# Top-32 attention with a channel mix: the mix cut into eighteen chunks of 256 rows instead of nineteen of four sizes, and the last batch walked in two passes over its heads instead of three

## The chip, the cores and the metric

The kernel runs on one core of a Trainium2 chip. The metric is device time in microseconds (us). The time before is the median of three runs; beside it stands one execution that was recorded by the hardware profiler. A core has TensorE (PE, matmuls; PEld is its weight load, which overlaps), VectorE (DVE), ScalarE (ACT), GpSimd (POOL) and SyncE (SP, which here only issues transfers).

## The reference, cut to what matters

```python
# B, H, S, D = 8, 8, 576, 64; d_model 512, d_ff 1024; all float32
scores = (q @ k.T) / 8                      # per batch and head, 576 x 576
kth    = 32nd largest of each row
attn   = softmax(where(scores >= kth, scores, -1e9))
x      = concat over heads of attn @ v      # B x 576 x 512
x_prev = x shifted down by one row, zero first
xk, xr = mu_k*x + (1-mu_k)*x_prev, mu_r*x + (1-mu_r)*x_prev
k      = relu(xk @ w_k)                     # 512 -> 1024
out    = sigmoid(xr @ w_r) * ((k*k) @ w_v)  # 1024 -> 512
```

`w_k`, `w_v`, `w_r`, `mu_k`, `mu_r` are shared by all batches; some of them arrive in 64 bits.

## The kernel before, in words

**Attention.** Heads go in four pairs `hp` of a batch. A pair's queries are cut into tiles numbered 0 to 8: tiles 0 to 7 come two by two (128 query rows for two heads), tile 8 holds the last 64 rows of both heads. That makes 288 tiles for 8 batches. For each tile PE computes scores (`score`, `sliver`, or `score8`, lines 957 to 974), ACT copies them out (`keep`), DVE finds the 32nd largest value with short maxima (`cand`, `best`, `drop`, `eighth`, `nine`) with the help of one ACT pass (`count`) and one POOL pass (`below`), ACT takes the exponential, DVE masks (`mask`), PE transposes (`turn`, `turnl`), ACT copies out, PE multiplies with v (`weigh`, L1048 and L1049), and DVE writes the normalised result into `xT[b]` (`place`, L1079 for two units of 128 rows at once, L1081 for one unit or for tile 8).

**Visits.** `visits()` lists (batch, pair, tiles). Normally a batch is walked in two passes, `HALVES = range(4), range(4, 9)`: tiles 0 to 3 of all four pairs, then tiles 4 to 8 of all four. `EDGE` gives the last batch three passes: tiles 0 to 3, 4 to 7, and 8 alone. Each visit loads and transposes the left-over rows (`load_t`, L898; `turn_t`, L930; `cr`, L932) and loads v (L903, L906). K itself is kept from one pass to the next (`HOLD`).

**Mix.** The 4608 rows (8 x 576, batches one after another) are cut into chunks by `SIZES`; a chunk may reach over a batch's end. For a chunk of n rows, POOL and ACT build the mixed inputs (`change` L1151, `share` L1156, `add` L1161, `xh` L1163, `xl` L1165), once for k and once for r, in two halves of two head pairs each. Every product runs as three matmuls, high by high, high by low, low by high (`three`, L688 to L690). `hidden` (L1172) puts weights in the array and moves n columns: 8 blocks x 4 x 3 = 96 matmuls per chunk, whatever n is. `relu`, `sq` (ACT), `r2`, `hl` (POOL) follow each pair of blocks. `gate` and `value` move 512 columns with up to 128 rows of the chunk as weights: 12 and 24 matmuls for each piece of up to 128 rows, so a chunk of 192 rows pays for two pieces. After the gates come `gexp` (ACT), `ga` (POOL L1199), `ln`, `inv1` (ACT), `newton` (POOL L1202), and after the values `scaled` and `gated` (DVE) and the store. In the last chunk `scaled` doesn't need the values (L1213).

**Which rows a chunk waits for.** `need` (L1133) lists the units of `xT` a chunk reads. Unit u is rows 128u to 128u+127 of a batch.

**Weights.** The 20 blocks of 128 x 512 are converted from 64 bits into a high and a low part (`weight`, L1236): one ACT, four DVE, two more ACT and one POOL step, and then for the first 12 blocks three-term sums on PE (`wsub`, with `ident` and a constant tile `minus`, the negative identity) and a copy on ACT (`wlo`), for the last 8 (the `v` blocks) two steps on POOL (L1270, L1271).

**Order.** Nothing is issued in program order. `Plan.op` registers each step with an engine, a cost and a key (a tile number plus `OFF[name]`, plus `HEAD[name]` for keys under `EARLY` = 48 and `TAIL[name]` for keys over `LATE` = 252); `Plan.run` plays the engines forward with these costs and picks on each engine the smallest key among the steps that can start soon. The result is a fixed order for every engine. A chunk's keys start at the later of 15.812 tiles per 256 rows after the chunk before and 10.811 tiles after the tile that completes its rows (lines 1128 to 1132). `piece` (L1120) chains all mix matmuls in order of chunks, and holds each until enough tiles have been scored.

```python
SIZES = [256] * 15 + [192, 256, 192, 128]
HALVES = range(4), range(4, 9)
EDGE = {B - 1: (range(4), range(4, 8), range(8, 9))}
```

Of the kernel before, what the change touches and what calls it, by code (L numbers as in the profile page):

```python
# [37 lines left out]
OFF = dict(kt=-21.783, kq=-11.008, rest=-13.373, v=-2.634, v8=10.138, tk=-6.089, ck=8.262, tq=-5.225, cq=-6.43, tr=-1.237, cr=-7.526, zero=22.403,  # L38
           score=-0.141, score8=-15.038, keep=-1.452, cand=4.806, best=-7.531, drop=-27.471, under=-2.738, nb=0.767, count=2.416, below=0.769,
           eighth=5.912, nine=7.69, exps=3.127, mask=1.266, turn=3.431, et=4.216, turnl=3.572, el=4.446, weigh=1.287, inv=2.357, inv2=-3.109,  # L40
           turni=-0.324, ri=1.01, place=-2.072, lowest=19.594, ranks=8.879, mu=-9.778, nmu=10.655, changek=8.233, sharek=-1.743, addk=-14.153,
           xhk=-0.414, xlk=-27.681, changer=-6.404, sharer=6.926, addr=3.569, xhr=6.702, xlr=-7.161, hidden=2.099, relu=-12.166, sq=4.501, r2=5.634,
           hl=-5.112, gate=1.899, gexp=6.101, ga=13.942, ln=-1.538, inv1=3.806, newton=-6.724, value=-0.034, scaled=-16.811, gated=-14.314,
           store=4.14, w=20.061, wabs=-2.342, wclamp=0.949, wshift=-6.042, wsign=-2.057, wexp=-2.168, wfine=1.502, whi=3.775, wmul=5.552,
           wsub=-10.606, wlo=3.473, spread=1.98, sliver=-2.472, low=4.289, lowt=-10.047, lowr=-8.942, lowc=-1.374)
# [21 lines left out]
SIZES = [256] * 15 + [192, 256, 192, 128]  # L67
# [4 lines left out]
BONUS = {("S", "W"): -0.314, ("T", "W"): 3.274, ("R", "W"): 3.937, ("T", "S"): -0.018, ("R", "S"): -0.24, ("W", "S"): -1.276, ("S", "R"): 1.995, ("T", "R"): -0.982, ("W", "R"): 4.176, ("R", "R"): -0.147}  # L72
# [331 lines left out]
def topk_attention_channel_mix(ctx: ExitStack, tc: tile.TileContext, q, k, v, mu_k, mu_r, w_k, w_v, w_r, out):  # L404
# [8 lines left out]
    minus = consts.tile([128, 128], F32R, name="minus")  # L413
    nc.vector.tensor_scalar(minus, ident, -1.0, None, op0=OP.mult)
# [7 lines left out]
    nmu = consts.tile([128, 2, HP], F32, name="nmu")  # L422
# [433 lines left out]
    def attend(plan, visits, X, pair_sums):  # L856
# [8 lines left out]
        for p, (b, hp, part) in enumerate(visits):  # L865
# [11 lines left out]
            P.q = {i: (buf("qn"), buf("qs")) for i in part if i % 4 == 0 and i < 8}  # L877
# [47 lines left out]
            for i, (qn, qs) in P.q.items():  # L925
                turned(qn, 2, lambda c, qn=qn: flat(qn.t[:, c]), "q", lambda qs=qs: qs.t, qs, at0 + i - P.first, fast=soon and i == 0)
# [14 lines left out]
            for i in part:  # L941
# [80 lines left out]
                if i % 2 or i == 8:  # L1022
# [28 lines left out]
                    plan.op(PE_, "weigh", n, cost, cost + 197, weigh, reads=[t.et for t in es] + [el] + [P.v, P.vr if i < 8 else P.vr8], writes=[U.pa[u]], mode="W")  # L1051
# [184 lines left out]
    def weight(plan, X, name, which, block, hi, lo, n):  # L1236
# [25 lines left out]
        if n < WPE:  # L1262
            pl = buf("rot")

            def rest():
                return [nc.tensor.matmul(pl.t, lhsT=minus if i == 1 else ident, rhs=x, start=i == 0, stop=i == 2) for i, x in enumerate((val.t, hi, fine.t))]
            plan.op(PE_, "wsub", key, 2050, 2250, rest, reads=[val, fine, (W, ('h', which))], writes=[pl], mode="T")
            done.append(plan.op(ACT, "wlo", key, 520, 630, lambda: nc.scalar.activation(lo, pl.t, AF.Copy), reads=[pl], writes=[(W, which)]))
        else:
# [147 lines left out]
```

## Time and profile before

| what | value |
|---|---|
| time, median of three runs | 1258.56 us (1258.01 to 1259.78) |
| the profiled execution's own time | 1260.28 us |
| its span | 1258.4 us |
| PE busy | 1204.9 us (96%) |
| DVE busy | 1136.3 us (90%) |
| ACT busy | 1114.2 us (89%) |
| POOL busy | 986.4 us (78%) |
| mean granted TensorE clock | 0.977 |

The span runs from the first to the last instruction on record; the time of the same execution is 1.88 us longer. Busy shares are means over a start in which weights are converted, a long stretch in which attention and mix run together, and an end in which only the mix is left, so they are to be read by stage. A matmul's recorded duration includes its way through the array; where matmuls follow one another, the distance between their starts is what each costs.

### The profile page before, as it was taken

To read this page: it belongs to the slowest core of one execution; us is meant where nothing else is said; L and a number is where in the kernel's file an instruction comes from. 1 tells how busy PE (TensorE), PEld (TensorE's weight loads), DVE (VectorE), ACT (ScalarE), POOL (GpSimd) and SP (SyncE) were. 2 spreads that over 40 slices of the span, in tenths; PEclk is the share of its full clock that TensorE was granted. 3 is DMA by queue.
4 is the path that set the end of the run, shared out by engine and by line. 5 is a ranking of instruction groups with operands and counts; after the bars stand their busy time and mean duration, and the time that the engine had idled before them with its cause. 6 is when DMAs were issued, how large, how long until landed. Compare 5 with 4: busy or idle time off the path is not lost.

```text
span 1258.4 us, 29994 instructions
## 1 busy us (share of the span) xinstructions
PE 1204.9 (96%) x9205; PEld 926.6 (74%) x9205; DVE 1136.3 (90%) x6219; ACT 1114.2 (89%) x2455; POOL 986.4 (78%) x885
## 2 busy tenths in 40 slices
PE   5786999999999999999999999999999999999998
PEld 3344777877777777777787877787878787778786
DVE  5999999999999999999999999999999999999101
ACT  5798899999999999999999999999999899999442
POOL 2558995987788887887888797978788879788783
PEclk8897799999999999999999999999999999999999
DMA  6233112111221112011211121112210211110100
GB/s 185 83 101 95 37 35 64 40 37 39 58 55 35 38 38 74 24 50 44 70 36 38 36 58 49 40 29 61 54 39 28 59 49 44 31 40 26 42 18 24
DMA packets 127257, 62.99 MB, mean 50 GB/s; under 512 B 102512, under 2 KB 119920, under 8 KB 127088
## 3 DMA queue, kind: packets, MB, share of 16 engines
q1 hardware_dynamic: 126400, 60.60, 17.8%
q8 instruction: 75, 1.23, 0.4%
q14 instruction: 94, 0.77, 0.2%
q10 hardware_dynamic: 688, 0.39, 0.1%
HBM read 51.52 MB, written 9.44 MB: 48 GB/s over the span
## 4 chain that ended last, share of the span: by engine, by line
PE 70%; ACT 12%; DVE 11%; issue 1%; POOL 1%; DMA 0%; POOLq 0%; DVEq 0%; ACTq 0%
PE rot L688 12%; PE rot L690 11%; PE rot L689 11%; PE ps L1048 9%; PE rot L1018 8%; PE ps L972 8%; DVE cand L982 2%; ACT sg L1002 2%; ACT sc L977 2%; ACT se L1010 2%; PE ps L968 2%; PE ps L959 2%; DVE E L1013 2%; PE ps L1049 2%; PE rot L917 2%; ACT et L1020 1%
## 5 line engine op out<-in xcount | busy, mean ns | idle before, releaser
L1004 POOL TENSOR_TENSOR sg<-sc,sg 128x576 f32<-128x576 f32 x288 | 409.4, 1423 | 173.5 <-ACT sg L1002 170.6
L982 DVE MAX8 cand<-sc 128x8 f32<-128x82 f32 (+1 forms) x2016 | 389.3, 231 | 10.8 <-ACT sc L977 9.5
L1002 ACT ACTIVATE sg<-sc,seen 128x576 f32<-128x576 f32 x288 | 225.6, 783 | 9.3 <-DVE seen L994 8.2
L1013 DVE SCALAR_TENSOR_TENSOR E<-sc,seen,se 128x576 f32<-128x576 f32 x288 | 231.2, 803 | 0.8 <-PE rot L1018 0.4
L1010 ACT ACTIVATE se<-sc,seen 128x576 f32<-128x576 f32 x288 | 217.7, 756 | 6.1 <-DVE E L1013 4.5
L1005 DVE MAX8 top<-sg 128x8 f32<-128x576 f32 x288 | 215.7, 749 | 2.5 <-POOL sg L1004 2.1
L977 ACT ACTIVATE sc<-ps 128x576 f32<-128x576 f32 x288 | 185.1, 654 | 25.7 <-PE ps L972 10.0
L1018 PE MATMUL rot<-ident,E 128*128 128x128 f32 x1152 | 182.3, 282 | 12.0 <-DVE E L1013 4.5
L984 DVE MAX8 top<-cand 128x8 f32<-128x56 f32 x864 | 179.9, 208 | 2.3
L1020 ACT ACTIVATE et<-rot 128x512 f32<-128x512 f32 x288 | 173.8, 603 | 8.9 <-PE rot L1018 7.7
L688 PE MATMUL rot<-xh,wk 128*128 128x256 f32 (+2 forms) x608 | 180.3, 297 | 0.4 <-ACT kd L932 0.4
L1018 PEld LDWEIGHTS rot<-ident,E 128*128 128x128 f32 x1152 | 132.8, 143 | 60.2 <-issue 6.5
L1048 PEld LDWEIGHTS ps<-et,v 128*64 128x64 f32 x2560 | 129.6, 139 | 55.9 <-ACT el L1029 14.9
L690 PE MATMUL rot<-xh,wk 128*128 128x256 f32 (+2 forms) x608 | 170.2, 280 | 0.0
L689 PE MATMUL rot<-xl,wk 128*128 128x256 f32 (+2 forms) x608 | 170.1, 280 | 0.0
L1048 PE MATMUL ps<-et,v 128*64 128x128 f32 (+1 forms) x2560 | 165.5, 272 | 4.1 <-ACT el L1029 3.8
L972 PE MATMUL ps<-K,qs 64*128 64x512 f32 x512 | 150.5, 666 | 0.0
L688 PE MATMUL rot<-wv,hh 128*128 128x512 f32 (+1 forms) x296 | 125.9, 425 | 0.5 <-ACT ri L1072 0.4
L688 PEld LDWEIGHTS rot<-xh,wk 128*128 128x128 f32 x608 | 116.4, 191 | 5.2 <-issue 2.0
L690 PE MATMUL rot<-wv,hl 128*128 128x512 f32 (+1 forms) x296 | 116.7, 394 | 0.0
L689 PEld LDWEIGHTS rot<-xl,wk 128*128 128x128 f32 x608 | 116.0, 191 | 0.1
L987 DVE MATCH_REPLACE8 cand<-top,cand 128x56 f32<-128x56 f32 x576 | 115.9, 201 | 0.0
(114 smaller groups left out, 2763.1 us busy)
## 6 DMA issues: line engine op xcount, KB each, us to landing
v<-in_v SPq DMA_DIRECT2D x68, 256.0 KB, 2.8
out<-eb SPq DMA_DIRECT2D x34, 256.0 KB, 2.1
kn<-in_k SPq DMA_DIRECT2D x64, 128.0 KB, 2.8
qn<-in_q SPq DMA_DIRECT2D x126, 64.0 KB, 2.1
stage<-in_moe_w_k SPq DMA_DIRECT2D x8, 512.0 KB, 6.1
xT<-in_moe_w_v SPq DMA_DIRECT2D x8, 512.0 KB, 3.6
tl<-in_k SPq DMA_DIRECT2D x136, 16.0 KB, 2.0
vr_in<-in_v SPq DMA_DIRECT2D x128, 16.0 KB, 2.4
```

What stands on the lines that cost most here:

```text
L688: return [nc.tensor.matmul(ps, lhsT=sh, rhs=mh, start=first, stop=False), nc.tensor.matmul(ps, lhsT=sh, rhs=ml, start=False, stop=False), ...
L689: nc.tensor.matmul(ps, lhsT=sh, rhs=ml, start=False, stop=False),
L690: nc.tensor.matmul(ps, lhsT=sl, rhs=mh, start=False, stop=last)]
L972: return [nc.tensor.matmul(ps[h].t, lhsT=qs.t[w, c * 128:(c + 1) * 128], rhs=P.K.t[w], start=True, stop=True) for h, w in enumerate(ws)]
L982: lambda T=T, c=c: nc.vector.max(T.cand.t[:, 8 * c:8 * c + 8], T.sc.t[:, CUTS[c]:CUTS[c + 1]]), reads=[T.sc], writes=[(T.cand, c)])
L1002: lambda T=T, sn=sn: nc.scalar.activation(T.side.t, T.sc.t, AF.Sign, bias=sn(T, 1), scale=-BELOW, accum_out=T.top.t[:, TOPK:TOPK + 1]),
L1004: plan.op(POOL, "below", n, 1375, 1430, lambda T=T: nc.gpsimd.tensor_mul(T.side.t, T.sc.t, T.side.t), reads=[T.sc], writes=[T.side])
L1005: plan.op(DVE, "eighth", n, 660, 754, lambda T=T: nc.vector.max(T.top.t[:, 24:32], T.side.t), reads=[T.side], writes=[(T.top, 3)])
L1010: plan.op(ACT, "exps", n, 667, 754, lambda T=T, pe=pe, sn=sn: nc.scalar.activation(pe.t, T.sc.t, AF.Exp, bias=sn(T, 0), scale=SCALE), read ...
L1013: lambda T=T, U=U, pe=pe, sn=sn: nc.vector.scalar_tensor_tensor(T.e(), T.sc.t, sn(T, 2), pe.t, op0=OP.is_ge, op1=OP.mult, accum_out=U.rs.t ...
L1018: return [nc.tensor.transpose(pt.t[:, c * 128:(c + 1) * 128], E.t[:, o + c * 128:o + (c + 1) * 128], ident) for c in range(NKC)]
L1048: return [*[nc.tensor.matmul(pa[hs[j]], lhsT=vs[j][:, c, :], rhs=ms[c][j], start=(c == 0), stop=False) for c in range(NKC) for j in range(2)],
```

## The change

`SIZES` becomes eighteen times 256. `EDGE` becomes empty, so that the last batch is walked in two passes like the others. All planner offsets get new values (`OFF`, `BONUS`, `CANDS`, `BESTS`, `WAT`, `WSTEP`, `GATE`, `VALUE`, two entries of `NEAR`, `LAG1`); `HEAD`, empty before, and `TAIL`, with one entry before, get one value for nearly each kind of step, so that steps near either end of the kernel have offsets of their own. Smaller edits: `nmu` shares the tile of `mu` and is computed in place; `minus` moves into the last block of `wv[1]`, so that the low parts of the `v` weights are ordered after the `wsub` sums that read it; the first half of a `gate` waits for its half of `xh` and `xl` only; some code paths are added that are switched off by the constants (`PAIR`, `WCL`) or that come to the same with the parts of a batch given here (the `m` of the q loads).

```diff
-OFF = dict(kt=-21.783, kq=-11.008, rest=-13.373, v=-2.634, v8=10.138, tk=-6.089, ck=8.262, tq=-5.225, cq=-6.43, tr=-1.237, cr=-7.526, zero=22.403,
...
-LAG, STEP, WAT, WSTEP, GATE, VALUE, PACE = 10.811, 15.812, 2.487, 0.785, 7.769, 14.051, -2.0
...
-EDGE = {B - 1: (range(4), range(4, 8), range(8, 9))}
...
+OFF = dict(kt=-21.382, kq=-14.248, rest=-18.039, v=-7.011, v8=8.546, tk=-6.103, ck=5.233, tq=-5.229, cq=-6.609, tr=-1.299, cr=-10.196, zero=24.959,
...
+LAG, STEP, WAT, WSTEP, GATE, VALUE, PACE = 10.811, 15.812, 0.678, 0.755, 7.749, 14.045, -2.0
...
+EDGE = {}
...
-SIZES = [256] * 15 + [192, 256, 192, 128]
+SIZES = [256, 256, 256, 256, 256, 256, 256, 256, 256, 256, 256, 256, 256, 256, 256, 256, 256, 256]
...
-HEAD = dict()
-TAIL = dict(addr=-0.777)
+HEAD = dict(sharek=3.354, ck=-3.568, zero=6.524, lowt=3.202, score8=0.214, ga=4.843, store=3.315, el=0.191, gate=0.108, wlo=0.364, tr=-0.131,
...
+TAIL = dict(addr=0.853, cr=4.328, wshift=-2.172, wexp=-2.611, scaled=0.049, sq=2.406, lowt=1.029, sliver=-0.332, nb=2.118, whi=1.277, xlk=6.06,
...
-    nmu = consts.tile([128, 2, HP], F32, name="nmu")
+    nmu = mu
...
-                    piece("gate", key(GATE + t // 64 + half), 6 * 231, gate, [xh, xl, *[(X.w["r"], (i, 0)) for i in range(half * HP // 2, (half + 1) * HP // 2)]], [pz])
+                    piece("gate", key(GATE + t // 64 + half), 6 * 231, gate, [(xh, half), (xl, half), *[(X.w["r"], (i, 0)) for i in range(half * HP // 2, (half + 1) * HP // 2)]], [pz])
...
-            done.append(plan.op(POOL, "wlo", key, 1258, 1310, lambda: nc.gpsimd.tensor_add(lo, val.t, fine.t), reads=[val, fine], writes=[(W, which)]))
+            done.append(plan.op(POOL, "wlo", key, 1258, 1310, lambda: nc.gpsimd.tensor_add(lo, val.t, fine.t), reads=[val, fine], writes=[(W, which)], after=X.subs if name == "v" else ()))
...
+        minus = wv[1][:, NFB - 1, :128]
+        nc.vector.tensor_scalar(minus, ident, -1.0, None, op0=OP.mult)
+        floor = late[:, 2176:2177].bitcast(F32)
+        nc.gpsimd.memset(floor, ZERO)
```

Rows to chunks: before, chunks 0 to 14 are 256 rows each, chunk 15 is the last 192 rows of batch 6, and batch 7 is rows 0 to 255 (chunk 16), 256 to 447 (17) and 448 to 575 (18). After, chunk 15 is those 192 rows of batch 6 and rows 0 to 63 of batch 7, chunk 16 is rows 64 to 319, chunk 17 rows 320 to 575.

## Rows read from the trace of the kernel before

**Rows 1.** The page, busy time of each engine.
```profile
PE 1204.9 (96%) x9205; PEld 926.6 (74%) x9205; DVE 1136.3 (90%) x6219; ACT 1114.2 (89%) x2455; POOL 986.4 (78%) x885
```

**Rows 2.** Six stretches: length, busy us of each engine (instructions), granted clock, DMA.
```profile
0.00:63.00 63.00, 42.40 (x138) 20.95 (x138) 47.95 (x196) 43.32 (x85) 23.14 (x29) 0.86 0.47 134
63.00:188.00 125.00, 106.75 (x736) 75.29 (x736) 123.27 (x623) 112.70 (x241) 104.97 (x89) 0.85 0.23 67
188.00:1164.00 976.00, 968.56 (x7738) 757.02 (x7736) 952.99 (x5378) 922.29 (x2053) 796.17 (x706) 1.00 0.17 45
1164.00:1180.00 16.00, 14.79 (x133) 10.80 (x132) 4.97 (x14) 7.44 (x19) 11.85 (x13) 1.00 0.26 81
1180.00:1243.00 63.00, 63.00 (x423) 54.94 (x422) 5.75 (x9) 25.76 (x54) 44.91 (x45) 1.00 0.05 16
1243.00:1258.40 15.40, 9.44 (x47) 7.63 (x46) 1.38 (x2) 2.67 (x5) 5.38 (x6) 0.91 0.06 22
```

**Rows 3.** PE in order of time: start, length, line, tiles, shape.
```profile
1184.09 0.28 PE L689 MATMUL rot<-xl,wk 128*128 128x256 f32 x1
...
1189.51 0.28 PE L690 MATMUL rot<-xh,wk 128*128 128x256 f32 x1
...
1206.13 0.25 PE L688 MATMUL rot<-xh,wk 128*128 128x192 f32 x1
...
1216.71 0.27 PE L690 MATMUL rot<-xh,wk 128*128 128x192 f32 x1
...
1233.34 0.22 PE L688 MATMUL rot<-xh,wk 128*128 128x128 f32 x1
...
1243.90 0.27 PE L690 MATMUL rot<-xh,wk 128*128 128x128 f32 x1
```

**Rows 4.** The end in order of time: ACT, DVE, the store's issue.
```profile
1247.02 0.60 ACT L1198 ACTIVATE eb<-rot 128x512 f32<-128x512 f32 x1 [1.92 <-PE rot L690]
...
1253.21 0.69 DVE L1214 SCALAR_TENSOR_TENSOR eb<-eb,rot 128x512 f32<-128x512 f32 x1
...
1253.93 0.37 ACTq L1221 DMA_DIRECT2D out<-eb  x1
```

**Rows 5.** DVE in order of time, the last results of attention.
```profile
1159.96 0.42 DVE L1079 TENSOR_TENSOR xT<-ps,ri 128x256 f32<-128x256 f32 x1
...
1184.08 0.23 DVE L1081 TENSOR_TENSOR xT<-ps,ri 128x64 f32<-128x64 f32 x1 [6.43 <-PE ps L1049]
```

**Rows 6.** POOL groups by shape, the mix of a 256-row chunk.
```profile
L1185 POOL TENSOR_TENSOR hl<-r,hh 128x512 fp32r<-128x512 f32 x64 | 82.3, 1286 | 5.0
L1165 POOL TENSOR_TENSOR xl<-xm,xh 128x512 fp32r<-128x512 f32 x64 | 82.1, 1287 | 4.7 <-ACT xh L1163 4.3
L1199 POOL TENSOR_SCALAR eb<-eb 128x512 f32<-128x512 f32 x35 | 67.2, 1921 | 4.8 <-ACT eb L1198 2.2
L1184 POOL TENSOR_TENSOR r<-r 128x512 f32<-128x512 f32 x64 | 66.6, 1041 | 13.7 <-ACT hh L1182 13.5
L1161 POOL TENSOR_TENSOR xm<-xm,xT 128x512 f32<-128x512 f32 x44 | 52.3, 1191 | 10.7 <-ACT xm L1156 10.6
L1202 POOL TENSOR_TENSOR eb<-eb,lb 128x512 f32<-128x512 f32 x35 | 45.2, 1291 | 5.2 <-ACT lb L1201 4.7
L1151 POOL TENSOR_TENSOR xd<-xT 128x512 f32<-128x512 f32 x22 | 22.9, 1043 | 0.0
```

**Rows 7.** ACT groups by shape: the scaling of a mix half, the k left-over copy.
```profile
L1156 ACT ACTIVATE xm<-xd,nmu 128x256 f32<-128x256 f32 x128 | 57.9, 515 | 0.3 <-POOL xd L1151 0.2
...
L932 ACT ACTIVATE kd<-rot 128x128 f32<-128x128 f32 x36 | 10.0, 276 | 0.9 <-PE rot L930 0.8
```

**Rows 8.** Single lines at the start: count, ns min/median/max, first and last start.
```profile
L688 PE MATMUL rot<-xh,wk x32: 276/281/562, 139.4 to 163.2; 128*128 128x256 f32 x32
L1271 POOL TENSOR_TENSOR wv<-eb,lb x8: 1264/1282/1465, 89.5 to 146.3; 128x512 fp32r<-128x512 f32 x8
L1266 PE MATMUL rot<-lb,ident x24: 591/592/1061, 33.4 to 80.9; 128*128 128x512 f32 x24
```

More of the change, by code (lines that the diff above doesn't have):

```diff
@@ L37 @@
 BIG = 3.0e38
-OFF = dict(kt=-21.783, kq=-11.008, rest=-13.373, v=-2.634, v8=10.138, tk=-6.089, ck=8.262, tq=-5.225, cq=-6.43, tr=-1.237, cr=-7.526, zero=22.403,
[L39 to L45, printed above, removed]
@@ L46 @@
-CANDS, BESTS = 0.043, -0.709
-LAG, STEP, WAT, WSTEP, GATE, VALUE, PACE = 10.811, 15.812, 2.487, 0.785, 7.769, 14.051, -2.0
-BACK, HOLD = False, 3
+OFF = dict(kt=-21.382, kq=-14.248, rest=-18.039, v=-7.011, v8=8.546, tk=-6.103, ck=5.233, tq=-5.229, cq=-6.609, tr=-1.299, cr=-10.196, zero=24.959,
+           score=-0.141, score8=-16.328, keep=-1.042, cand=4.797, best=-8.27, drop=-27.489, under=-2.864, nb=-4.48, count=2.291, below=0.265,
+           eighth=6.343, nine=7.479, exps=3.115, mask=-0.613, turn=3.366, et=4.204, turnl=3.568, el=4.37, weigh=1.271, inv=3.182, inv2=-5.081,
+           turni=-0.009, ri=0.848, place=-1.878, lowest=20.12, ranks=16.635, mu=-6.363, nmu=11.593, changek=8.781, sharek=-2.615, addk=-15.155,
+           xhk=-0.563, xlk=-31.338, changer=-9.67, sharer=8.479, addr=2.956, xhr=5.904, xlr=-8.649, hidden=2.062, relu=-10.213, sq=4.638, r2=6.141,
+           hl=-4.223, gate=1.884, gexp=5.081, ga=14.727, ln=-4.806, inv1=3.806, newton=-5.08, value=-0.042, scaled=-17.152, gated=-15.006,
+           store=7.854, w=19.648, wabs=-0.882, wclamp=0.952, wshift=-8.969, wsign=-1.393, wexp=-0.548, wfine=1.179, whi=3.694, wmul=8.819,
+           wsub=-8.872, wlo=4.08, spread=1.597, sliver=-4.179, low=2.901, lowt=-13.42, lowr=-9.695, lowc=-4.212, wcp=0.231)
@@ L49 @@
+CANDS, BESTS = 0.045, -0.62
+LAG, STEP, WAT, WSTEP, GATE, VALUE, PACE = 10.811, 15.812, 0.678, 0.755, 7.749, 14.045, -2.0
+BACK = False
+HOLD = 3
+PAIR = False
+WCL = 0
 HALVES = range(4), range(4, 9)
-EDGE = {B - 1: (range(4), range(4, 8), range(8, 9))}
+EDGE = {}
 def visits():
@@ L71 @@
 SWITCH = {("T", "T"): 10, ("T", "S"): 92, ("T", "Z"): 10, ("T", "W"): 92, ("T", "R"): -50, ("R", "R"): 0, ("R", "T"): 85, ("R", "S"): 165, ("R", "Z"): 80, ("Z", "T"): 60, ("Z", "S"): 92, ("Z", "W"): 150, ("Z", "R"): -35, ("R", "W"): 165, ("W", "W"): 10}
-BONUS = {("S", "W"): -0.314, ("T", "W"): 3.274, ("R", "W"): 3.937, ("T", "S"): -0.018, ("R", "S"): -0.24, ("W", "S"): -1.276, ("S", "R"): 1.995, ("T", "R"): -0.982, ("W", "R"): 4.176, ("R", "R"): -0.147}
+BONUS = {("S", "W"): -1.086, ("T", "W"): 3.287, ("R", "W"): 3.489, ("T", "S"): -0.028, ("R", "S"): -0.426, ("W", "S"): -1.169, ("S", "R"): 1.769, ("T", "R"): -0.968, ("W", "R"): 4.451, ("R", "R"): -0.294}
 LEAVE = dict(S=95, W=103)
@@ L75 @@
 WINDOW, PHASE, WARM, COLD = 3413.0, 2079.0, 0.87, 0.58
-NEAR = dict(PE=182, ACT=168, DVE=28, POOL=271, SP=302)
+NEAR = dict(PE=182, ACT=165, DVE=28, POOL=271, SP=294)
 LAST, JOINT, PEAT = "last", True, 112
 LWAT, LWSTEP = -2.585, 1.51
-LAG0, LAG1 = 8.92, 22.884
+LAG0, LAG1 = 8.92, 24.398
 WPE = 12
-HEAD = dict()
-TAIL = dict(addr=-0.777)
+HEAD = dict(sharek=3.354, ck=-3.568, zero=6.524, lowt=3.202, score8=0.214, ga=4.843, store=3.315, el=0.191, gate=0.108, wlo=0.364, tr=-0.131,
+            turni=-1.056, sq=3.388, ln=-4.07, hl=-5.431, changer=2.017, relu=-14.934, wmul=-1.439, low=4.872, xhk=0.716, inv=2.094, v=4.81,
+            gated=-1.266, xlk=12.101, turn=0.113, r2=0.637, xlr=-10.187, inv1=4.923, addr=1.519, ri=-4.935, below=-1.831, scaled=-5.097, best=-1.072,
+            wabs=-0.847, lowr=-0.696, sliver=-1.103, tk=-0.128, nmu=-3.551, kq=3.958, changek=2.107, count=-0.05, hidden=-1.273, addk=-5.101,
+            xhr=2.146, lowc=-0.428, cq=0.701, eighth=-1.645, w=1.074, nb=-2.325, kt=-7.062, wshift=-2.765, wexp=0.003, ranks=8.978, rest=-10,
+            spread=5.051, mask=-0.34, whi=0.196, newton=-10.373, drop=-2.508, gexp=-0.274, keep=-0.268, tq=-0.017, inv2=3.214, mu=-5.036, weigh=0.017,
+            cr=-1.986, turnl=0.004, score=-0.211, under=-2.424, v8=2.951, nine=0.151, place=1.785, sharer=3.985, et=0.015, wfine=-0.129, wsign=1.009,
+            exps=-0.306, wsub=-1.021, lowest=-1.465, value=0.017, wcp=-0.278)
@@ new lines @@
+TAIL = dict(addr=0.853, cr=4.328, wshift=-2.172, wexp=-2.611, scaled=0.049, sq=2.406, lowt=1.029, sliver=-0.332, nb=2.118, whi=1.277, xlk=6.06,
+            xhk=3.07, store=0.534, nine=0.364, best=-3.303, wclamp=-3.212, ck=-0.471, rest=7.98, lowr=3.739, ln=-0.612, hl=2.336, turni=-5.416,
+            xhr=-5.491, relu=-1.983, kt=0.597, v8=1.982, drop=-9.156, gate=-0.048, score8=3.803, eighth=1.269, under=5.06, inv2=2.762, v=0.064,
+            w=-0.347, wmul=-2.191, wfine=2.635, cq=-0.832, lowest=-2.842, gexp=0.175, score=0.034, sharek=-1.259, wabs=-0.36, exps=0.582, nmu=-3.842,
+            below=0.883, changek=2.733, tr=2.248, lowc=-0.397, tq=-0.647, wsub=1.611, inv=-0.862, low=2.896, gated=1.923, turnl=-0.233, place=1.226,
+            ri=-4.487, r2=5.335, weigh=1.024, spread=-7.381, kq=3.792, cand=0.342, value=0.124, hidden=-0.65, newton=5.24, changer=2.918, zero=1.577,
+            ranks=-4.862, mu=2.617, count=2.536, mask=4.85, tk=1.419, wsign=0.085, xlr=3.997, wlo=-3.068, inv1=-0.011, keep=-0.009, addk=4.321,
+            ga=1.91, el=0.034, sharer=-1.07, wcp=0.415, turn=-0.048)
@@ L412, in topk_attention_channel_mix @@
     make_identity(nc, ident)
-    minus = consts.tile([128, 128], F32R, name="minus")
-    nc.vector.tensor_scalar(minus, ident, -1.0, None, op0=OP.mult)
     ranks_i = consts.tile([128, 9], I32, name="ranks_i")
@@ L876, in attend @@
                 held[b, hp] = P.K
-            P.q = {i: (buf("qn"), buf("qs")) for i in part if i % 4 == 0 and i < 8}
+            P.q = {i: (buf("qn"), buf("qs")) for i in part if i < 8 and (i % 4 == 0 or i == P.first)}
+            P.qs = {i: max(j for j in P.q if j <= i) for i in part if i < 8}
             soon = p == 0
@@ L887, in attend, with load_q @@
                 issue = nc.scalar if now else nc.sync
-                def load_q(b=b, hp=hp, i=i, qn=qn, issue=issue):
+                m = list(P.qs.values()).count(i) // 2
+                def load_q(b=b, hp=hp, i=i, qn=qn, issue=issue, m=m):
                     for h in range(2):
-                        issue.dma_start(qn.t[:, :, h, :], q[b, 2 * hp + h, i * 64:i * 64 + 256].rearrange("(c p) d -> p c d", p=128))
+                        issue.dma_start(qn.t[:, :m, h, :], q[b, 2 * hp + h, i * 64:i * 64 + m * 128].rearrange("(c p) d -> p c d", p=128))
                 plan.op(ACT if now else SP, "kq", at0 + i - P.first, 1000, 2700, load_q, writes=[qn])
@@ L925, in attend @@
             for i, (qn, qs) in P.q.items():
-                turned(qn, 2, lambda c, qn=qn: flat(qn.t[:, c]), "q", lambda qs=qs: qs.t, qs, at0 + i - P.first, fast=soon and i == 0)
+                m = list(P.qs.values()).count(i) // 2
+                turned(qn, m, lambda c, qn=qn: flat(qn.t[:, c]), "q", lambda qs=qs, m=m: qs.t[:, :m * 128], qs, at0 + i - P.first, fast=soon and i == 0)
             pt, m = buf("rot"), 1 + full
@@ L948, in attend @@
                     U.i = i
-                    U.rs = buf("rs")
+                    U.rs, U.weigh = buf("rs"), []
                     U.w = 1 if i == 8 else min(part[-1], i | 3) + 1 - i
@@ L963, in attend @@
                     ps, sl = [buf("psA"), buf("psB")], buf("sl")
-                    qs, c = P.q[i // 4 * 4][1], i // 2 % 2
+                    qs, c = P.q[P.qs[i]][1], (i - P.qs[i]) // 2
                     def sliver(P=P, sl=sl, qs=qs, c=c):
@@ L1050, in attend @@
                     cost = 1140 if i < 8 else 629
-                    plan.op(PE_, "weigh", n, cost, cost + 197, weigh, reads=[t.et for t in es] + [el] + [P.v, P.vr if i < 8 else P.vr8], writes=[U.pa[u]], mode="W")
+                    U.weigh.append((weigh, cost, [t.et for t in es] + [el], U.pa[u]))
+                    if not PAIR or u == (U.w - 1) // 2:
+                        fs, cs, rs, ws = zip(*U.weigh)
+                        U.weigh = []
+                        plan.op(PE_, "weigh", n, sum(cs), sum(cs) + 197, lambda fs=fs: [x for f in fs for x in f()], reads=[x for r in rs for x in r] + [P.v, P.vr if i < 8 else P.vr8], writes=ws, mode="W")
                 if i % 4 == 3 or i == part[-1]:
@@ L1226, in weights @@
         buf = plan.buf
-        X.staged, X.late = [], []
+        X.staged, X.late, X.subs = [], [], []
         X.w = {c: buf("w" + c) for c in "rkv"}
@@ L1251, in weight @@
         o = plan.op(SP, "w", key, 600, 4500, lambda: nc.sync.dma_start(st.t.rearrange("p c t -> p (c t)"), block.bitcast(U32)), writes=[st])
-        plan.op(ACT, "wabs", key, 552, 640, lambda: nc.scalar.activation(pm.t, high().bitcast(F32), AF.Abs), reads=[st], writes=[pm, (val, "held")])
-        plan.op(DVE, "wclamp", key, 588, 692, lambda: nc.vector.tensor_scalar(pm.t, pm.t, ZERO, None, op0=OP.max), writes=[pm])
-        plan.op(DVE, "wshift", key, 588, 692, lambda: nc.vector.tensor_scalar(U(pm), U(pm), 3, 0x3FFFFFFF, op0=OP.logical_shift_left, op1=OP.bitwise_and), writes=[pm])
+        if n < WCL:
+            plan.op(ACT, "wabs", key, 552, 640, lambda: nc.scalar.activation(val.t, high().bitcast(F32), AF.Abs), reads=[st], writes=[val])
+            plan.op(POOL, "wcp", key, 1235, 1290, lambda: nc.gpsimd.tensor_max(val.t.bitcast(I32), val.t.bitcast(I32), X.floor.bitcast(I32).to_broadcast([128, 512])), writes=[val])
+            plan.op(DVE, "wshift", key, 588, 692, lambda: nc.vector.tensor_scalar(U(pm), U(val), 3, 0x3FFFFFFF, op0=OP.logical_shift_left, op1=OP.bitwise_and), reads=[val], writes=[pm])
+        else:
+            plan.op(ACT, "wabs", key, 552, 640, lambda: nc.scalar.activation(pm.t, high().bitcast(F32), AF.Abs), reads=[st], writes=[pm, (val, "held")])
+            plan.op(DVE, "wclamp", key, 588, 692, lambda: nc.vector.tensor_scalar(pm.t, pm.t, ZERO, None, op0=OP.max), writes=[pm])
+            plan.op(DVE, "wshift", key, 588, 692, lambda: nc.vector.tensor_scalar(U(pm), U(pm), 3, 0x3FFFFFFF, op0=OP.logical_shift_left, op1=OP.bitwise_and), writes=[pm])
         plan.op(DVE, "wsign", key, 588, 692, lambda: nc.vector.scalar_tensor_tensor(U(val), high(), 0xC0000000, U(pm), op0=OP.bitwise_and, op1=OP.bitwise_or), reads=[st, pm], writes=[val])
@@ L1265, in rest @@
             def rest():
-                return [nc.tensor.matmul(pl.t, lhsT=minus if i == 1 else ident, rhs=x, start=i == 0, stop=i == 2) for i, x in enumerate((val.t, hi, fine.t))]
-            plan.op(PE_, "wsub", key, 2050, 2250, rest, reads=[val, fine, (W, ('h', which))], writes=[pl], mode="T")
+                return [nc.tensor.matmul(pl.t, lhsT=X.minus if i == 1 else ident, rhs=x, start=i == 0, stop=i == 2) for i, x in enumerate((val.t, hi, fine.t))]
+            X.subs.append(plan.op(PE_, "wsub", key, 2050, 2250, rest, reads=[val, fine, (W, ('h', which))], writes=[pl], mode="T"))
             done.append(plan.op(ACT, "wlo", key, 520, 630, lambda: nc.scalar.activation(lo, pl.t, AF.Copy), reads=[pl], writes=[(W, which)]))
@@ L1316, in graph @@
             X = Env()
+            X.minus, X.floor = minus, floor
             X.ranks, X.least, X.mu = plan.buf("ranks"), plan.buf("least"), plan.buf("wmu")
```

## The prediction, made before the changed kernel was run

> **What bounds the kernel now.** I read the page's busy line first [rows 1]: PE 96%, DVE 90%, ACT 89%. These are means, so I split the span by stage [rows 2]. There are four stages. Up to 188 us PE is busy for 42.40 + 106.75 = 149.2 of 188 us, so it idles 38.9 us, and the granted clock is 0.85 to 0.86; DVE is full from 63 us on (123.27 of 125), because it also converts the weights. From 188 to 1164 us PE (968.56 of 976, 99.2%) and DVE (97.6%) are both full at full clock. From 1164 us DVE has next to nothing to do, and PE alone works off a backlog of mix matmuls: 1.2 us idle to 1180, none at all to 1243. In the last 15.4 us it works for 9.4 and waits for the last transfer.
>
> So the end is set by PE's total work: while attention lasts PE has no room, and what it couldn't do by 1164 us takes it 87 us more. Whatever is taken off PE anywhere after 188 us, and is not replaced by a wait, comes off the end. The attention itself is paced by DVE, and it ends near 1164 us whatever PE has left over.
>
> **Hidden matmuls.** In the tail PE runs unbroken, so starts can be subtracted [rows 3]. With 256 columns: 1184.09 to 1189.51 is 46 steps, 0.1178 us each, 11.31 us for a chunk's 96. With 192 columns: 1206.13 to 1216.71 is 95 steps, 0.1114 us each, 10.69 us. With 128: 1233.34 to 1243.90 is 95 steps, 0.1112 us each, 10.67 us. A chunk with half the columns costs 94% as much. The last four chunks (192, 256, 192, 128) therefore cost 2 x 10.69 + 11.31 + 10.67 = 43.4 us, the three of 256 after the change 33.9 us: **-9.4 us**.
>
> The Trainium skill ("TensorE: Matmul & The Clock Gate", section "Back-to-back issue gap") gives an isolated matmul a gap of columns over 2.4 GHz plus 2.5 ns, which would make a 128-column matmul half as dear as one of 256; by it the four chunks would cost as much as the three, and this term would be nothing. The rows disagree: 0.1112 us at 128 columns. The same page ("LDWEIGHTS") makes a load of 128 weight columns last 107 ns, close to the step seen.
>
> **Gates and values.** They go by pieces of up to 128 rows, 36 matmuls each. Between the 192-row chunk's last hidden matmul (1216.71) and the next chunk's first (1233.34) lie its 72, so 16.63 less one hidden step of 0.11 is 16.52 us, 0.229 each [rows 3]. The second piece of that chunk has only 64 rows and pays in full. Before, the last four chunks have 2 + 2 + 2 + 1 = 7 pieces, after, three chunks have 6: one piece less, **-8.3 us**.
>
> **Passes.** Four visits vanish. All tiles stay. Each vanished visit took one transpose of the left-over k rows and its copy, 0.28 us on ACT (36 such copies, of which 32 stay [rows 7]), plus loads of v and left-over rows. The transpose costs PE about a hidden step, 4 x 0.11: **-0.4 us**. The copies (1.1 us of ACT) and loads are off the path: ACT has idle time in every stage [rows 2], and DMA is at most a quarter busy after 188 us; without that cover the copies would be worth 1.1 us.
>
> **The end.** Before, the last gate ends at about 1247.0, and gexp, ga, ln, inv1, newton, scaled and gated follow one another to 1253.9, when the store is issued; 4.5 us later the span ends [rows 4]. The values behind that gate were done by about 1252.4 (1243 plus 9.44 busy [rows 2]), so PE's last 1.5 us to the store were spent waiting for the gate chain. After the change the last gate is followed by 11 us of values (two pieces) instead of 5.5; the chain of 6.2 us to `gated` is under them, and only gated (0.69) and the store remain: 5.2 us behind PE's end instead of 6.0. **-0.8 us**.
>
> **What the larger tail chunks add.** POOL's work for one 256-row chunk [rows 6]: 2 change, 4 add, 4 xl, 4 r2, 4 hl, 2 ga, 2 newton = 2.1 + 4.8 + 5.1 + 4.2 + 5.1 + 3.8 + 2.6 = 27.7 us. PE's is 11.3 + 16.5 = 27.8 us. In the pure tail two such chunks now run with nothing else, and POOL keeps step only if it loses nothing. Before, POOL was busy 44.9 of 63 us there [rows 2]. The k inputs of chunk 17 have to be made within chunk 16's 27.8 us, but most of its ga and newton can slip. Below, this costs nothing; above, a whole k preparation laid bare between the chunks (2 change, 2 add, 2 xl) is 7.0 us. As POOL runs beside PE elsewhere in the tail, I take **+1.0 us**, near the low end.
>
> **The small edits.** `nmu` in place is the same single DVE step. The move of `minus` makes the low v weights wait for the sums: the last sum starts at 80.9 us and the first low v weight at 89.5 [rows 8], 8.6 us of cover; without it each us would delay the first values, not PE's total. The half-wise gate wait can only help, by no more than a POOL step (1.29 us) per chunk, and PE has no idle there to gain. All at nothing.
>
> **The new offsets.** They reorder every engine. Between 188 and 1164 us PE idles 7.4 us in all [rows 2], so a better order there is worth at most that on PE. At the start there is more: 38.9 us of PE idle, and 15.1 us of DVE idle in the first 63 us. The weights' keys start 1.8 tiles earlier. DVE must wait for the first loads anyway (it is full from 63 us), so I bound the start at 8 us either way and take zero.
>
> **Sum.** -9.4 - 8.3 - 0.4 - 0.8 + 1.0 = -17.9 us. Against the profiled execution's 1260.28 that is 1242.4; that execution lies 1.7 us above the median of the runs, so the forecast is **1240.7 us**.
>
> **Is the work there to be done?** With the new cut both chunk 16 (rows 64 to 319) and chunk 17 need the last visit: its tiles 4 to 7 for the one, tile 8 for the other. Before, only 320 rows waited for the last passes. The last result of tiles 4 to 7 is written at 1159.96 [rows 5]. From there change, share (two of 0.515 [rows 7]), add, xh and xl take about 5.5 us, so chunk 16 may begin at about 1166 to 1168; two chunks of 27.8 and 5.2 us behind PE's end give 1227 to 1229 as the earliest possible span. PE's total gives 1240.5, so 12 us of slack remain, filled by the rest of chunk 15. Before, the last write at 1184.08 plus 5 us of inputs, 10.7 + 2.8 us of matmuls, the 6.9 us chain and 4.5 us gave a floor near 1214, with 44 us of slack. The change eats most of that reserve.
>
> **Rivals.**
> *Attention ends later (the slower case).* The two chunks that hang on the last visit and their inputs take 66 us behind it. If its tile-7 result comes later than about 1172, the end moves one for one; at 1190 all of the gain is gone, and beyond it the kernel is slower. 30 us is 3.1% of the 976 us in which DVE is 97.6% busy: an order in which DVE's share falls to 94.7% is enough. For it: every offset is new, and mix and attention wait in the same queues. Against: DVE's work is the same, and its share has stayed at that level for the whole stretch. At a share of 94.2%, 36 us late, the time is about 1264. Chance 0.12 for slower, 0.04 for an end within 0.2% of before, and 0.08 for a delay that costs 5 to 15 us (1246 to 1256).
> *POOL holds the tail.* A bare k preparation of 7 us, and perhaps one more for the second chunk's low parts: 1246 to 1253. For it: 27.7 against 27.8 us. Against: chunk 16's r inputs can be made under chunk 15's values. Chance 0.06.
> *Matmuls go by their columns.* Then only the piece of gates and values is saved: 1250. The three steps in [rows 3] speak against it; 0.02. This is what the page's gap formula would have come to.
> *The start gets shorter too.* If 5 to 10 us of PE's idle at the start go, 1231 to 1236. The granted clock there, 0.85 on the mean of its levels 1.2 and 2.4 GHz, could rise too. Chance 0.12.
> *The forecast*, 1236 to 1246: 0.56.
>
> **Numbers.** The range 1231 to 1253 leaves out the slower case, most of the same and a little on either side, some 0.2. A change under 0.2% (2.5 us, about what runs of this kernel can tell) is called the same. Faster: 0.56 + 0.12 + 0.08 + 0.06 + 0.02 = 0.84; same 0.04; slower 0.12.
>
> **What would show it.** The changed profile should have 576 + 144 + 288 instead of 608 + 148 + 296 matmuls at each of the three mix lines, about 18 us less PE work, PE unbroken from attention's end to the last values, and gated directly behind the last value. DVE should fall silent near 1164 us. Idle of PE between chunk 16's values and chunk 17's hidden, released by POOL, would show the POOL case; PE idle ahead of chunk 16's first hidden matmul, the late attention; a first hidden matmul far from 139.4 us [rows 8], the start. The forecast fails if the new order costs DVE's share more than a per cent.

## The result and the profile after

The changed kernel takes 1239.57 us (1238.81 to 1239.90) against 1258.28 for the kernel before in the same session: ratio 0.9849, interval 0.9837 to 0.9861, 18.7 us less. The forecast was 1240.7.

The page's busy line and six stretches, columns as in [rows 2]:

```profile
PE 1185.3 (96%) x9069; PEld 913.8 (74%) x9069; DVE 1132.4 (91%) x6217; ACT 1107.8 (89%) x2428; POOL 980.6 (79%) x872
...
0.00:63.00 63.00, 45.02 (x171) 23.19 (x172) 49.93 (x204) 44.90 (x89) 23.63 (x31) 0.89 0.50 139
63.00:188.00 125.00, 102.67 (x720) 72.09 (x720) 123.01 (x628) 112.61 (x243) 106.51 (x90) 0.88 0.23 65
188.00:1164.00 976.00, 969.97 (x7761) 760.10 (x7760) 947.11 (x5363) 919.33 (x2040) 795.83 (x708) 1.00 0.17 44
1164.00:1180.00 16.00, 16.00 (x128) 13.78 (x127) 5.80 (x18) 9.92 (x23) 12.82 (x13) 1.00 0.09 34
1180.00:1222.00 42.00, 42.00 (x256) 37.29 (x256) 2.77 (x4) 19.51 (x35) 38.12 (x31) 1.00 0.04 13
1222.00:1238.00 16.00, 9.62 (x42) 7.39 (x40) 3.81 (x4) 1.50 (x3) 3.65 (x3) 0.92 0.11 38
```

PE's work behind 1164 us is 16.00 + 42.00 + 9.62 = 67.6 us; it was 14.79 + 63.00 + 9.44 = 87.2 [rows 2]. That is where the gain shows: 19.6 us less there, 1.4 more from 188 to 1164, 1.5 less ahead of 188. PE is unbroken from 1164 us to its end, and POOL is 91% busy from 1180 to 1222 (38.12 of 42).

PE in order of time in the tail, columns as in [rows 3] (first hidden matmul of chunk 16, its first gate, the same two of chunk 17):

```profile
1175.07 0.28 PE L703 MATMUL rot<-xh,wk 128*128 128x256 f32 x1
...
1186.46 0.40 PE L703 MATMUL rot<-wr,xh 128*128 128x512 f32 x1
...
1203.27 0.28 PE L703 MATMUL rot<-xh,wk 128*128 128x256 f32 x1
...
1214.66 0.40 PE L703 MATMUL rot<-wr,xh 128*128 128x512 f32 x1
```

Chunk 16 starts at 1175.07 and chunk 17 at 1203.27. But 96 hidden matmuls take 11.39 us and 72 gate and value matmuls 16.81, where 11.31 and 16.52 were read before.

DVE, POOL and ACT's store in order of time: what chunk 16, chunk 17 and the end waited for.

```profile
1168.28 0.41 DVE L1101 TENSOR_TENSOR xT<-ps,ri 128x256 f32<-128x256 f32 x1
...
1231.65 0.69 DVE L1236 SCALAR_TENSOR_TENSOR eb<-eb,rot 128x512 f32<-128x512 f32 x1 [3.96 <-PE rot L705]
```
```profile
1173.75 2.55 POOL L1187 TENSOR_TENSOR xl<-xm,xh 128x512 fp32r<-128x512 f32 x2
...
1201.48 2.56 POOL L1187 TENSOR_TENSOR xl<-xm,xh 128x512 fp32r<-128x512 f32 x2
```
```profile
1232.37 0.37 ACTq L1243 DMA_DIRECT2D out<-eb  x1
```

The last result of tiles 4 to 7 (L1101, the old L1079) is written at 1168.28, 8.3 us later than before [rows 5]. The first of the two `xl` that begin at 1173.75 ends at about 1175.0, and chunk 16's first hidden matmul starts at 1175.07. For chunk 17 that step ends at about 1202.7, half a us ahead of PE. So PE waits for nothing, but nothing is to spare either.

### The profile page after: what moved, and what is told of

The parts are those of the page before. It is cut to its first block, busy times and chain, and to the rows that moved or that the text cites. A ratio compares the mean times of both kernels' runs of the same rounds, so it can differ in the third digit from the quotient of the medians.

```text
span 1238.0 us, 29646 instructions
## 1 busy us (share of the span) xinstructions
PE 1185.3 (96%) x9069; PEld 913.8 (74%) x9069; DVE 1132.4 (91%) x6217; ACT 1107.8 (89%) x2428; POOL 980.6 (79%) x872
## 3 DMA queue, kind: packets, MB, share of 16 engines
HBM read 50.34 MB, written 9.44 MB: 48 GB/s over the span
## 4 chain that ended last, share of the span: by engine, by line
PE 79%; DVE 9%; ACT 6%; issue 1%; POOL 0%; DMA 0%; SPq 0%; DVEq 0%; ACTq 0%
PE rot L703 13%; PE rot L705 12%; PE rot L704 12%; PE ps L1066 10%; PE rot L1036 9%; PE ps L990 9%; PE ps L986 2%; PE ps L1067 2%; PE ps L977 2%; PE rot L934 2%; DVE cand L1000 2%; DVE E L1031 2%; PE rot L1088 1%; ACT sc L995 1%; PE ps L1045 1%; ACT se L1028 1%
## 5 line engine op out<-in xcount | busy, mean ns | idle before, releaser
L995 ACT ACTIVATE sc<-ps 128x576 f32<-128x576 f32 x288 | 185.4, 653 | 27.8 <-DVE E L1031 11.4
L703 PE MATMUL rot<-xh,wk 128*128 128x256 f32 x576 | 172.5, 299 | 0.4 <-ACT kd L950 0.4
L1066 PEld LDWEIGHTS ps<-et,v 128*64 128x64 f32 x2560 | 128.7, 138 | 54.5 <-ACT el L1047 17.9
L705 PE MATMUL rot<-xh,wk 128*128 128x256 f32 x576 | 162.4, 282 | 0.0
L704 PE MATMUL rot<-xl,wk 128*128 128x256 f32 x576 | 162.1, 281 | 0.0
L703 PE MATMUL rot<-wv,hh 128*128 128x512 f32 x288 | 123.3, 428 | 0.0
L705 PE MATMUL rot<-wv,hl 128*128 128x512 f32 x288 | 113.7, 395 | 0.0
L704 PE MATMUL rot<-wv,hh 128*128 128x512 f32 x288 | 113.6, 394 | 0.0
L703 PEld LDWEIGHTS rot<-xh,wk 128*128 128x128 f32 x576 | 109.7, 190 | 5.0 <-issue 2.4
```

The lines of the kernel that those rows point to most:

```text
L703: return [nc.tensor.matmul(ps, lhsT=sh, rhs=mh, start=first, stop=False), nc.tensor.matmul(ps, lhsT=sh, rhs=ml, start=False, stop=False), ...
L704: nc.tensor.matmul(ps, lhsT=sh, rhs=ml, start=False, stop=False),
L705: nc.tensor.matmul(ps, lhsT=sl, rhs=mh, start=False, stop=last)]
L1066: return [*[nc.tensor.matmul(pa[hs[j]], lhsT=vs[j][:, c, :], rhs=ms[c][j], start=(c == 0), stop=False) for c in range(NKC) for j in range(2)],
```

## The experiments

Each was timed beside the kernel before. "Later tiles" are those that are allocated behind `mu`.

**Which part carries the gain.** Four kernels.

```diff
 e1 = before with
+SIZES = [256] * 18
+EDGE = {}
+    piece("gate", ..., gate, [(xh, half), (xl, half), ...
```


> The kernel before with the new cut (eighteen chunks of 256, two passes in the last batch) and its own old offsets; the half-wise wait of the gates is taken over too. If the gain is PE work taken off the last four chunks (18 us, the forecast's theory), nearly all of it is here: 1239 to 1244 us, and PE busy about 18 us below the 1204.9 of before. If the new offsets carry a good part of it (the rival), this stays at 1248 us or above, with PE idle in front of the last two chunks.

Measured: 1239.21 us, 19.5 below before (ratio 0.9845, 0.9829 to 0.9862). The cut, with the half-wise wait of the gates, carries the whole gain; that wait was not run by itself. PE was busy for 1181.1 us, 23.8 less than before, where about 18 was expected. The two profiled executions lie 22.3 us apart, 2.8 more than the medians, which is part of that miss; the rest is open.

e2 is e1 without the line for `EDGE`, so with three passes.


> The kernel before with eighteen chunks of 256, but still three passes in the last batch, old offsets, half-wise gate wait. PE-work theory: the saving of hidden, gate and value matmuls (17.7 us) is all here, the four visits (0.4 us) are not: 1240 to 1244 us. If two passes were needed to feed the last chunks in time, 1248 us or more.

Measured: 1243.28 us (0.9877, 0.9861 to 0.9894). The sizes are worth 15.4 us, the two passes, on top of the new sizes, 4.1 more, ten times the 0.4 of the forecast. In the stretches from 1100 us on, PE has gaps that the changed kernel hasn't:

```profile
1100.00:1164.00 64.00, 61.49 (x490) 48.59 (x487) 59.55 (x328) 57.55 (x128) 53.77 (x49) 1.00 0.12 35
1164.00:1181.00 17.00, 15.32 (x122) 11.62 (x121) 4.14 (x10) 8.96 (x23) 13.56 (x14) 1.00 0.18 57
```

2.5 and 1.7 us of idle, in several waits of under 1 us (a load of left-over rows, the `ri` and `el` copies of short visits). Each short visit brings its own chain of small steps. The kernel before has three passes too, and in the same stretches PE idles for only 0.1 us (63.91 of 64 busy) and 1.2 us [rows 2]: there PE's backlog of mix work covers these waits. So the 4.1 us hold beside the new sizes; two passes with the old sizes were not run.

e3 is the changed kernel with the old `SIZES` and `EDGE`.


> The changed kernel with the old cut (short chunks at the end, three passes): the new offsets and small edits alone. PE-work theory: within 5 us of before, 1253 to 1263 us. If the offsets carry the gain: 1250 us or less.

Measured: 1259.61 us (1.0009, 0.9999 to 1.0018). Offsets and small edits together give nothing.

```diff
 e4 = after with
+HEAD, TAIL = {}, {}
 e12 = after with
+TAIL = {}
```


> The changed kernel with empty offsets for both ends, so that the general offsets hold from start to end. PE-work theory: 1237 to 1245 us, as PE's work is the same and only idle time can change. If the offsets of the ends are what keeps PE fed at the start and in the tail: 1247 us or more, with the added idle of PE before 188 us or in front of chunks 16 and 17.

> The changed kernel with its offsets for the start kept and those for the tail emptied. Without both it took 1251.2 us, with chunk 16's hidden matmuls from 1186.8 instead of 1175.1. If the tail's offsets are what brings the last visit's results early enough: 1246 us or more and a start of chunk 16 at 1182 or later. If the start's are: 1238 to 1243 us.

Measured: e4 1251.19 us, 11.6 above the changed kernel; e12 1240.81, 1.2 above. So the start's offsets matter, and the tail's hardly. In e4 the last visit's result comes at 1177.56 instead of 1168.28, and PE is busy for 963.8 us of the 976 from 188 on, against 970.0. The general offsets were used together with those of the start; this says what taking those away costs, not what the start could gain over before. Why a changed start is still felt 700 us later is open.

**What a hidden matmul costs.**

```diff
 e5 = after with
+SIZES = [256] * 8 + [128, 128] + [256] * 9
```


> The changed kernel with its ninth chunk of 256 rows cut into two of 128: as many gate and value matmuls, 96 more hidden ones, all 192 of them with half the columns. If a hidden matmul costs 0.111 us at 128 columns and 0.118 at 256, this adds 96 x (2 x 0.1112 - 0.1178) = 10.0 us: 1249 to 1251 us. If a matmul goes by its columns, next to nothing is added: 1239 to 1241 us.

Measured: 1258.14 us, 18.6 above the changed kernel, more than either expectation. PE's busy time rose by 10.8 us (1196.1 against 1185.3), near the 10.0 by rows. By the gap formula for an isolated matmul in the Trainium skill ("TensorE: Matmul & The Clock Gate", section "Back-to-back issue gap"), which goes by columns, it would by estimate hardly have risen; the trace disagrees. The other 7.8 us is idle: the new order has PE busy for 963.6 us of the 976 from 188 on, and the last result of tiles 4 to 7 comes at 1186.57.

**Whether there is slack behind the last visit.** In tile 7 of the last visit:

```diff
-nc.vector.max(T.top.t[:, 24:32], T.side.t)
+[nc.vector.max(T.top.t[:, 24:32], T.side.t) for _ in range(13)]
```


> The changed kernel with one maximum of the very last pair of tiles (eighth, in tile 7 of the last visit) done 13 times instead of once, without the planner knowing: the order is the same, and the last visit's results come about 12 x 0.66 = 8 us later. If 12 us of slack lie behind the last visit, as forecast: within 1.5 us of the changed kernel, 1239 to 1241 us. If there is none, as the changed kernel's trace suggests (chunk 16's first hidden matmul starts in the moment its inputs are ready): 6 to 9 us more, 1245 to 1249 us, with PE idle in front of it.

> The same 12 extra maxima, with their cost told to the planner, which may put other work in their place. If slack is a matter of order (work of chunk 15 that can be kept back for the wait): 0 to 4 us more than the changed kernel, 1239 to 1244 us. If PE has nothing left to fill the wait: as much as with the unknown delay, 1245 to 1249 us.

Measured: e6 1251.02 us, e7 1253.55, so 11.5 and 14.0 us more. DVE and PE of e6 in order of time, and its stretch around the delay:

```profile
1162.18 10.31 DVE L1024 MAX8 top<-sg 128x8 f32<-128x576 f32 x13 [0.50 <-POOL sg L1022]
...
1179.61 0.42 DVE L1102 TENSOR_TENSOR xT<-ps,ri 128x256 f32<-128x256 f32 x1
```
```profile
1173.77 1.09 PE L1037 MATMUL rot<-ident,E 128*128 128x128 f32 x4 [9.06 <-DVE E L1032]
...
1177.43 0.49 PE L1089 MATMUL rot<-ident,ri 128*128 128x128 f32 x2
...
1186.49 0.28 PE L703 MATMUL rot<-xh,wk 128*128 128x256 f32 x1
```
```profile
1168.00:1177.00 9.00, 3.23 (x10) 2.78 (x11) 6.61 (x15) 2.03 (x4) 1.14 (x2) 0.50 0.00 0
```

The same two places of PE's order in the changed kernel:

```profile
1164.18 0.60 PE L1036 MATMUL rot<-ident,E 128*128 128x128 f32 x4
...
1166.12 0.38 PE L1088 MATMUL rot<-ident,ri 128*128 128x128 f32 x2
```

The maxima cost 9.6 us more. PE idled for 9.06 us ahead of the transposes, and from 1168 to 1177 us the granted clock was 0.50, the lower of its two levels (1.2 and 2.4 GHz). The Trainium skill ("TensorE: Matmul & The Clock Gate", section "Part 1: The HAM clock gate") has an idle PE throttled to half its clock; this trace agrees. The transposes and the six values behind the idle took 3.66 us (1173.77 to 1177.43) instead of 1.94 (1164.18 to 1166.12). So the 9.6 us became 11.3 at the visit's result, 11.4 at chunk 16 and 11.5 at the end: there is no slack at all in this order, and a fifth comes on top by the clock.

Telling the planner didn't help. PE of e7:

```profile
1176.31 1.12 PE L1037 MATMUL rot<-ident,E 128*128 128x128 f32 x4 [4.76 <-DVE E L1032]
...
1186.39 0.38 PE L703 MATMUL rot<-xh,wk 128*128 128x256 f32 x1 [1.98 <-ACT xh L1186]
```

It put values ahead of the delayed transposes, so that PE waited 4.76 us there instead of 9.06. Those values were then missing while chunk 16's inputs were made, and PE waited again: chunk 16's hidden matmuls took 16.7 us (1183.42 to the first gate at 1200.15) instead of 11.4. The work that can fill the wait is used up either way.

**The small edits.**

```diff
 e8 = after with
-    nmu = mu
+    nmu = consts.tile([128, 2, HP], F32, name="nmu")
-        minus = wv[1][:, NFB - 1, :128]
+        minus = one.tile([128, 128], F32R, name="minus")
-    after=X.subs if name == "v" else ()
```


> The changed kernel with tiles of their own for nmu and minus again, and the low v weights no longer ordered after the sums; the half-wise gate wait stays. Expected at nothing: within 1.5 us of the changed kernel, 1238 to 1241 us. If sharing those tiles had a price at the start: 2 us or more below it.

Measured: 1234.42 us (0.9812, 0.9796 to 0.9828), 5.1 below the changed kernel and faster than both. All engines issue the same steps in the same order. What differs is where tiles lie: without `nmu`, 32 bytes per partition, every later tile starts 32 bytes off. Three more runs test this.

```diff
 e9 = after, e10 = e1, each with a tile of 32 bytes (e11 = after, 96 bytes)
+    pad = consts.tile([128, 8], F32, name="pad")
+    nc.gpsimd.memset(pad[:1, :1], 0.0)
     least = consts.tile([128, B + 1], F32, name="least")
```


> The changed kernel with one unused tile of 32 bytes per partition behind mu, so that all later tiles (K, E, xh, xl, hh, hl and so on) start at multiples of 64 bytes again instead of 32 past one; nmu still shares mu's tile and minus the v weights'. In the run with tiles of their own for nmu and minus, a run of 72 gate and value matmuls took 16.40 us instead of the changed kernel's 16.81, and 96 hidden ones 11.30 instead of 11.39. If the address is the cause: the same 16.40 and 11.30, and 1233 to 1236 us. If sharing the tiles is: 16.81 and 11.39, and 1238 to 1241 us.

> The kernel before with the new cut and its old offsets (which took 1239.2 us, with 16.40 us for 72 gate and value matmuls), and the same unused tile of 32 bytes, which here moves the later tiles off multiples of 64. If the address is the cause: about 16.8 us for the 72 and 1243 to 1248 us. If not: 1238 to 1241 us.

> The changed kernel with an unused tile of 96 bytes: later tiles start at multiples of 64 that are not multiples of 128. If multiples of 64 are enough: as with 32 bytes, 16.4 us for 72 gate and value matmuls and 1233 to 1236 us. If it takes multiples of 128: 16.8 us and 1238 to 1241 us.

| run | start of `xh`, `xl`, modulo 128 bytes | start of `hh`, `hl`, modulo 128 | 96 hidden, us | 24 gate, us | 48 value, us | time, us |
|---|---|---|---|---|---|---|
| e1, before's offsets | 0 | 64 | 11.30 | 5.52 | 10.88 | 1239.21 |
| e10, e1 shifted by 32 | 32 | 96 | 11.35 | 5.61 | 11.19 | 1243.72 |
| the changed kernel | 96 | 32 | 11.39 | 5.61 | 11.20 | 1239.57 |
| e8, tiles of their own | 0 | 64 | 11.30 | 5.52 | 10.88 | 1234.42 |
| e9, 32 bytes of padding | 0 | 64 | 11.31 | 5.51 | 10.88 | 1234.49 |
| e11, 96 bytes of padding | 64 | 0 | 11.50 | 5.46 | 11.20 | 1239.97 |

The start addresses are those in the built programs. The later tiles don't share one residue, as the expectations above have it: two `xT` tiles that take up 9248 bytes each lie between `xl` and `hh`, so that `hh` and `hl` lie 64 further, and `K` starts at 96 in e9. `wk`, `wv` and `wr` are allocated ahead of `mu` and start at 64 in all six programs. The times of matmuls are differences of starts, as for e9 and e11 here (first hidden, gate and value of chunk 16, first hidden of chunk 17):

```profile
1170.98 0.28 PE L705 MATMUL rot<-xh,wk 128*128 128x256 f32 x1
...
1182.29 0.40 PE L705 MATMUL rot<-wr,xh 128*128 128x512 f32 x1
...
1187.80 0.39 PE L705 MATMUL rot<-wv,hh 128*128 128x512 f32 x1
...
1198.68 0.28 PE L705 MATMUL rot<-xh,wk 128*128 128x256 f32 x1
```
```profile
1174.79 0.28 PE L705 MATMUL rot<-xh,wk 128*128 128x256 f32 x1
...
1186.29 0.40 PE L705 MATMUL rot<-wr,xh 128*128 128x512 f32 x1
...
1191.75 0.40 PE L705 MATMUL rot<-wv,hh 128*128 128x512 f32 x1
...
1202.95 0.28 PE L705 MATMUL rot<-xh,wk 128*128 128x256 f32 x1
```

Padding by 32 bytes removes 5.1 us; the same padding adds 4.5 us where the tiles lay well. The address is the cause; sharing the tiles costs nothing.

## Why the prediction was right, and where its steps failed

The forecast's total was met, and its theory of PE work is borne out by e1. But that the total came within 1.1 us is in part luck. Two terms that the forecast took at nothing cancelled: on well placed tiles the new offsets are worth 1239.2 - 1234.5 = 4.7 us (e1 against e9), and the 32 bytes take 5.1 back. And the sizes gave 15.4 us (e2) where the forecast's terms for them (-9.4 - 8.3 - 0.8 + 1.0) make 17.5, while the passes gave 4.1 instead of 0.4.

- *Hidden matmuls (-9.4) and gates and values (-8.3).* The counts are as forecast (576 hidden, 144 gate, 288 value at each of the three lines). With e1, where nothing but the cut and the half-wise wait changed, the sum of the terms, -17.9, came out as -19.5. The durations in the changed kernel were longer than the rows of before, by 0.08 and 0.29 us per chunk; against e1, whose tiles lie better, it is 0.09 and 0.41.
- *Passes (-0.4).* Mis-sized: -4.1 between e2 and e1. What was missing is PE's small waits around short visits, which stay uncovered once the new sizes have taken work off PE (e2).
- *The end (-0.8).* `gated` does follow the last value directly (1231.65). But the span ended 5.6 us behind the store's issue (1232.37 to 1238.0) instead of 4.5, so PE's end to the span's end is 6.4 us, 0.4 more than before. Other runs lay between 4.4 (e3) and 6.0 (e4); why was not tested.
- *Larger tail chunks (+1.0).* Cost nothing: PE is unbroken. POOL was busy for 27.2 of the 27.7 us between the `xl` of chunk 16 and that of chunk 17, much as sized; PE's chunk took 28.2 instead of 27.8 us, and POOL came in half a us ahead of it.
- *Small edits (nothing).* Failed: 5.1 us, by the address and not by any wait that was looked at.
- *New offsets (zero, 8 us either way).* 4.7 us, within the bounds.
- *Twelve us of slack.* Failed: there was none. The step took the 1159.96 of before for the result of tiles 4 to 7 in the last visit. That time belongs to three passes, in which all four tiles 8 come behind it. In two passes the tiles 8 of the first three pairs come ahead of it (written at 1118.43, 1137.25 and 1156.54), and it came at 1168.28. The lines below, of e2 and then e1, which differ in the passes alone, show it move by 7.1 us.

```profile
1157.44 0.43 DVE L1079 TENSOR_TENSOR xT<-ps,ri 128x256 f32<-128x256 f32 x1 [0.26 <-ACT el L1029]
```
```profile
1164.53 0.42 DVE L1079 TENSOR_TENSOR xT<-ps,ri 128x256 f32<-128x256 f32 x1 [1.63 <-ACT el L1029]
```

  So chunk 16 began at 1175.07 instead of 1166 to 1168, two chunks and the end took 63.0 us instead of 60.8, and the span ended at 1238.0 instead of 1240.5: together that is the 12. The slower rival's price was therefore too kind: it let this result come as late as 1172 for nothing, but a delay costs from its first us (in e6 11.3 us at the result, 11.5 at the end). That DVE's share fell from 97.6 to 97.0% didn't show, as PE was full all the same. Attention's last write came at 1172.59, so DVE fell silent later than near 1164.

## What to carry to other kernels

Price matmuls by the distance of their starts in the trace: here 128 columns cost 94% of 256, so that a cut into equal full chunks is worth the instructions it saves. When a cut moves more work behind the last input, measure the reserve by delaying that input, not by subtracting times of the old order. After any edit to allocations, compare the step of unchanged matmuls: a few bytes can hide or fake a gain as large as the planner's.

## What the runs showed of the hardware that was not expected

TensorE's step depends on where its operands start in SBUF. In the gate and value matmuls the moving operand (`wr`, `wv`) had the same address with and without padding, so of their two operands it is the loaded one (`xh`, `xl`, `hh`, `hl`) that counts. With it at 64 past a multiple of 128 bytes, 48 value matmuls took 10.88 us; at 0, 32 or 96 past, 11.19 to 11.20 (3% more). 24 gate matmuls took 5.46 us at 64, 5.51 to 5.52 at 0, and 5.61 at 32 and 96. In the hidden matmuls the loaded weights stayed and the moving operand shifted: 96 took 11.30 us at 0, 11.35 at 32, 11.39 at 96, and 11.50 at 64, so that the best place for one use is the worst for the other. Gates and values don't agree at 0, so the start modulo 128 is not the whole rule; what the rule is, and whether the distance to the other operand counts, stays open. In the kernel before, with the residues of e1, the 24 gates of chunk 16 took 5.60 us and the 48 values 10.91, and that difference in the gates is open as well.

A version that beats both kernels is the changed kernel with 32 bytes of padding, or with a tile of its own for `nmu` and `minus`: 1234.5 us.
